# Sigmoid attention and token mixing on one core: a new written-out order, and copies split by PSUM bank

## The chip, the core and the metric

The kernel runs on one core of one Trainium2 chip. The metric is device time in microseconds (us) of one execution. A profile of one execution gives a span, from the first to the last instruction of the program; the execution's own time is a little longer. Engines are TensorE (PE in the profile, with its weight loads as PEld), VectorE (DVE), ScalarE (ACT), GpSimd (POOL) and SyncE (SP), whose queue issues nearly all transfers.

## What is computed

Batch 8, 12 heads, 448 tokens, head size 64, model width 768. Attention with a sigmoid in place of a softmax feeds a token mixer:

```
scores = scale * q @ k.T - log(448);  attn = sigmoid(scores);  x = attn @ v        # per head, x is (8, 448, 768)
wq, wk = x @ w_q, x @ w_k                                                          # (8, 448, 64)
W_tok  = scale * wq @ wk.T;  mixed = W_tok @ x
out    = relu(mixed) @ w_out                                                       # (8, 448, 768)
```

The kernel never forms W_tok: it multiplies wk by x first, a 64 by 768 matrix per batch entry ("tmp"), and that by wq.

## The kernel before, in words

Four heads of one batch entry make a quad; there are 24 quads, three for each of the eight batch entries u. For each quad q, k and v are loaded (448 KB each), cast to bf16 and, for q and k, transposed. The casts are mostly on POOL (L192, L202); the transposes are 32x32 block transposes on DVE (L232, L256, L263, with swaps of halves on POOL, L161 to L167) or matmuls with an identity (L216, L224).

Each quad has seven score steps S (`scores`, L294): four 64x64 matmuls of 448 columns that run side by side in the array's four quarters (L298), into two PSUM banks, and one sigmoid on ACT over 896 columns (L303). Seven value steps P (L320) accumulate attn times v; the last of them copies the sum out as xt (L329). A step x (`tr_x`, L342 or L358) transposes xt back into xn.

When the three quads of u are done the mixer of u follows: W (`mlp_wqk`), six products of xt and the two projection weights, either over the whole 128x128 array (L395, with a second copy wq by POOL or ACT at L404 or L402) or over its four quarters (L383, with two copies and an addition, L390 to L392); N, transposes of wk (L410); U or T, tmp (L424, or L439 in quarters, L443 and L444); M (`mlp_mix`, L463 or L474) and a relu on the way out of PSUM (`relu`, L446: ACT at L448 or DVE at L450). Then the output products O and I with w_out, in pairs w of batch entries: for w in TW = (1, 2) `out_pair` (quarters, L506, one copy out at L515); for w = 0 and 3 `out_chunk` (whole array, six matmuls to a half row block, L583, copy at L607) or `out_halves` (quarters, L542, L547 and L548). Outputs are stored from SP (L523, L556, L592).

Nothing of the order is left to a scheduler. `PLAN` (L132) is a string of 636 letters that the loop at L761 walks: S is a score step, P or p a value step, O or o a step of an output product, and so on; a small letter mostly puts the copy on ACT in place of DVE, and other letters choose other forms (`ALIKE`, L757). Every engine executes its instructions in the order in which the loop emits them. `BANKS` (L67) names the PSUM bank or pair of banks for each step that needs one. `ORDER` (L657) is the order of 77 loads: "w0" is the two projection weights, "w1" to "w6" the six blocks of the output weights. Loads go through a ring of eight buffers (`pump_loads`, L676), so a load is issued once the tile eight places before it in the ring has been cast; casts are given to POOL in the same order as soon as their buffers allow (`pump`, L717), save for the entries marked with a dot or a capital, which DVE or ACT takes (letters 1 and 2 in `PLAN`). The output weights are cast at L704.

Two letters decide where a copy runs:

```
read(fb, COPY["s" if act else "v"](out=o, in_=ps[:, :, 0:NB]), keep=True)    # out_pair: one engine, both banks
tail = done["S"] == N * NI                                                     # after the last score step
```

After the last score step `tail` is true, and then `values`, `tr_x` and the relu of `mlp_mix` outside TW split each copy by bank, one half on DVE and one on ACT.

Of the kernel before, what the change touches and what calls it, by code (L numbers as in the profile page):

```python
# [17 lines left out]
def kernel(  # L18
# [17 lines left out]
    P = 128  # L36
# [4 lines left out]
    NB = D // 2  # L41
# [6 lines left out]
    def pool(name, bufs, **kw):  # L48
# [16 lines left out]
    banks16 = banks.rearrange("p b x -> p (b x)").bitcast(BF16).rearrange("p (b x) -> p b x", b=8)  # L65

    BANKS = (  # L67
# [11 lines left out]
    )  # L79
    BANKS = BANKS.split()[::-1]  # L80

# [43 lines left out]
    def xt(u, j):  # L125
# [4 lines left out]


    PLAN = (  # L132
        "FFSSSKSSFaSbFFrSFFSFsFzFSSPSSpPpPpPpSSrSsPppSSPPPSxzSSSXSPrP"
        "SpSsPPPPzSWwwWSSwWXSPPNrpSppSPPSUSPSszSpppSqkpSpPSMSSMSxSxSM"
        "cdSPppPSSpPPWrSwWsWSSWWPpSXSPPpSPzPSOSOSxNSOSrsSOoSSOTzSSppp"
        "ppSSpProoSpSPpSPPpSsPWwzWoSWMSWoWSSMoOSNxSPcPSMPppSPdPSoCCOS"
        "SScXOCOSpdppSxCpPSpCPSUrSPPSPpSPPPSszoOSSSCOoXwwwSMSWoWSxSWO"
        "SMSpppcSppSdPPPcPpSPpPSPSoONSMSooxdSTSPPPSppPSPSOYoWWWWw1WSM"
        "OSocSONdSOmppppcpSoSpPdOSOSOSXXSmooSo1TcoSooSMOSOPPSPSpppSdP"
        "cOoSooMSPpPPp2SpPSWXWwwwWXmOSOSodOSOSoSocpSPOpSPdPSPPOSoSONS"  # L140
        "OSUSOS1MoSOMoPmpcdPPpPSPo1SOSoSOoSOxSoSOPSPppScPdSpOPOSoxSOc"
        "lLSlSlLLOdSOSoxSOppPSNppPSPpPSpppSPpTOSOSoxSOPPmpPpMPPmxWWWw"
        "wwxiNiitiiimmiiIMiIiOOoOOoOooOOooOoO"
    )
    KIND = ["a"] + [t for t in PLAN if t in "qacer"]

# [226 lines left out]
    wkn, tmps, mxs = {}, {}, {}  # L373
# [72 lines left out]
    def relu(fb, dst, ps, act):  # L446
        if act:
            inst = nc.scalar.activation(dst, ps, ACTF.Relu, bias=0.0, scale=moe_scale)  # L448
        else:
            inst = nc.vector.tensor_scalar(dst, ps, moe_scale, 0.0, ALU.mult, ALU.max)  # L450
        read(fb, inst)

    def mlp_mix(u, c, act, tail):
        w = u // 2
        if c == 0 and u % 2 == 0:
            mxs[w] = p_mx.tile([P, 2 * 12 * 256], BF16, tag="mx", name="mx")
        fb, ps, _ = bank2()
        wq = (wqks[u % 2], wq2s[u % 2])
        if w in TW:
            for z in range(2):  # L460
                for y in range(2):
                    for x in range(2):
                        nc.tensor.matmul(  # L463
                            ps[HALF[x], y, 256 * z : 256 * z + 256],
                            tmps[u][HALF[y], c * P + 64 * z : c * P + 64 * z + 64],
                            wq[y][HALF[y], 192 * x : 192 * x + 256], start=True, stop=True,
                        )
            relu(
                fb, mxs[w].rearrange("p (u y c x) -> p u c y x", u=2, y=2, c=3)[:, u % 2, c], ps, act
            )  # L470
            return
        for y in range(2):
            for x in range(2):
                nc.tensor.matmul(  # L474
                    ps[HALF[x], y, 0:S], tmps[u][HALF[y], c * P + 64 * x : c * P + 64 * x + 64],
                    wq[y][HALF[y], 0:S], start=True, stop=True,
                )
        mx = mxs[w][:, 0 : 12 * S].rearrange("p (y c u s) -> p c u y s", y=2, c=3, u=2)[:, c, u % 2]
        if tail:
            for y in range(2):  # L480
                relu(fb, mx[:, y], ps[:, y, 0:S], y)
        else:
            relu(fb, mx, ps[:, :, 0:S], act)
# [7 lines left out]

        return b // 2 + (0 if b % 2 == half else NC)

    def out_pair(act):

        if opened:
            w, blocks, part, fb, ps = opened.pop()
        else:
            w, blocks = chunks.pop(0)
            part = 0  # L500
            fb, ps, _ = bank2()
        mx = mxs[w].rearrange("p (u b x) -> p u b x", u=2, b=12)
        for b in range(3 * part, 3 * part + 3):
            for y, (u, i) in enumerate(blocks):
                for x in range(2):
                    nc.tensor.matmul(  # L506
                        ps[HALF[x], y, 0:NB], mx[HALF[y], u, b, 64 * (i - 3 * y) : 64 * (i - 3 * y) + 64],
                        wout16[HALF[y], slot(y, b), x * NB : (x + 1) * NB],
                        start=(b == 0), stop=(b == 11),
                    )  # L510
        if part < 3:
            opened.append((w, blocks, part + 1, fb, ps))
            return
        o = p_o.tile([P, 2, NB], F32, tag="o", name="o")
        read(fb, COPY["s" if act else "v"](out=o, in_=ps[:, :, 0:NB]), keep=True)  # L515
        (u0, i0), (u1, i1) = blocks
        for x in range(2):
            cols = slice(x * NB, (x + 1) * NB)
            if u0 == u1:
                dst = out[2 * w + u0].rearrange("(p i) d -> p i d", i=NI)[:, i0 : i1 + 1 : i1 - i0, cols]  # L520
            else:
                dst = out[2 * w : 2 * w + 2].rearrange("b (p i) d -> i p b d", i=NI)[i0, :, :, cols]
            nc.sync.dma_start(out=dst, in_=o[HALF[x]])  # L523
# [129 lines left out]
    for t in wqks:  # L653
# [1 line left out]


    ORDER = (  # L657
# [4 lines left out]
    )  # L662
    BY = {"s": [], "v": []}
    for x in ORDER.split():
# [89 lines left out]
    used |= {("q", 0), ("k", 0)}  # L754
    pump()

    ALIKE = dict(a="q", c="q", e="q", r="q", b="k", d="k", f="k", s="k", j="k", h="k", X="x", y="x", Y="x", g="g", z="z", L="W", l="W", T="U", t="U", I="O", i="O")  # L757
    done["q"] = done["k"] = 1
    quads_r = []

    for t in PLAN:  # L761
# [11 lines left out]
            scores(*divmod(c, NI))  # L773
        elif kind == "P":
            n, i = divmod(c, NI)
            values(n, i, tail, "s" if t == "p" else "v")
            if i == NI - 1:
                used.add(("v", n))
                pump()
# [11 lines left out]
        elif t == "g":  # L791
            move()
        elif t == "z":
            n = quads_r.pop(0)
            quadrants(n, 1)
            used.update({("q", n), ("k", n)})
            pump()
        elif t == "K":
            tr_part("k", k016, KB, "v")
        elif kind == "x":  # L800
            tr_x(c, tail, t in "XY", "s" if t in "yY" else "v")
        elif kind == "W":
            mlp_wqk(*divmod(c, NC), tail, t in "wl", t in "Ll")
        elif kind == "C":
            for y in range(2):
                nc.sync.dma_start(out=wout16[HALF[y], NC + c, :], in_=wout16[HALF[1 - y], c, :])
        elif kind == "N":
            mlp_wkn(c)
        elif kind == "U":
            (mlp_tmp_tiled if t in "Tt" else mlp_tmp)(c, t in "ut")  # L810
        elif kind == "M":
            u, x = divmod(c, NC // 2)
            mlp_mix(u, x, t == "m", tail)
            if x == NC // 2 - 1:
                if u // 2 in TW:
                    chunks.extend((u // 2, ((u % 2, i), (u % 2, 6 - i))) for i in range(3))
                    if u % 2:
                        chunks.append((u // 2, ((0, 3), (1, 3))))
                else:
                    chunks.extend((u // 2, m, -1) for m in (range(3, NI) if u % 2 else range(3)))  # L820
        elif kind == "O":
            if (opened or chunks)[0][0] in TW:
                out_pair(t == "o")
            elif t in "Ii":
                out_halves(t == "i")
            else:
                out_chunk(t == "o", tail)
    assert not chunks and not opened and not BANKS
# [1 line left out]
_INS = ['q', 'k', 'v', 'moe_w_q', 'moe_w_k', 'moe_w_out']  # L830
# [26 lines left out]
```

## Time and profile before

| what | us |
|---|---|
| median of three runs | 186.23 (184.76 to 186.94) |
| the profiled execution's own time | 185.52 |
| its span | 183.7 |
| busy: PE, ACT, DVE, POOL | 171.8, 162.0, 143.3, 125.3 |
| first sigmoid starts, last sigmoid ends | 7.04, 160.94 |
| loads and stores: moved, mean rate | 48.47 MB, 264 GB/s |

The granted TensorE clock was full (1.00) over the whole span. A line of the groups gives the source line, engine, operation, tiles (out<-in), shape and count, then busy time in us, the mean of one in ns and the idle time of the engine before them with what ended it. A busy PE is not a PE at its peak, since the ends of pipelined matmuls are modelled; four quarter matmuls that run side by side count once in busy time.

### The profile page before, as it was taken

Reading aid. Unit: us, or ns where it says so; the run is one execution under the profiler, and the core shown is the slowest. Engines: PE = TensorE matmul, PEld = TensorE weight load, DVE = VectorE, ACT = ScalarE, POOL = GpSimd, SP = SyncE. Lnnn points to the kernel's source line nnn. Section 1 sums busy time; section 2 is a strip of 40 time slices with the busy share of each in tenths; the row PEclk is TensorE's granted clock in tenths of the full one; section 3 lists DMA queues with packets and bytes.
Section 4 is the critical chain, followed back from the end, with each engine's and each line's share of the span. In section 5 each row is a group of like instructions: output and inputs, shape, how many; then the busy total and the mean of one; then the engine's idle time right before and its main releaser. Section 6 shows DMA issues by size and latency. Waiting matters only on the chain.

```text
span 183.7 us, 7643 instructions
## 1 busy us (share of the span) xinstructions
PE 171.8 (94%) x3313; PEld 111.0 (60%) x3314; DVE 143.3 (78%) x221; ACT 162.0 (88%) x208; POOL 125.3 (68%) x168
## 2 busy tenths in 40 slices
PE   7877799979999999999999999999999999999990
PEld 7433445444545446555665887867766778878650
DVE  3229999999999999888987976876587788596720
ACT  4599999999999989999999999999999999977330
POOL 1399887999972999999998999996999921000000
PEclk9999999999999999999999999999999999999999
DMA  5999999959999947898998778999759534231786
GB/s 175 332 404 397 324 343 403 397 192 329 364 409 386 340 131 266 274 305 259 316 295 269 207 268 241 390 372 370 227 127 304 171 92 107 69 88 27 177 232 171
DMA packets 24722, 48.47 MB, mean 264 GB/s; under 512 B 3952, under 2 KB 17264, under 8 KB 24688
## 3 DMA queue, kind: packets, MB, share of 16 engines
q1 hardware_dynamic: 24288, 47.20, 78.5%
q10 hardware_dynamic: 400, 0.79, 1.4%
q8 instruction: 26, 0.43, 0.9%
q14 instruction: 8, 0.07, 0.1%
HBM read 35.78 MB, written 11.01 MB: 255 GB/s over the span
## 4 chain that ended last, share of the span: by engine, by line
PE 64%; DVE 16%; ACT 10%; DMA 4%; POOL 1%; SPq 1%; issue 1%
PE banks L506 15%; PE banks L298 12%; PE banks L320 11%; ACT at L303 10%; PE banks L583 10%; DVE qk L232 6%; DMA q<-in_q_dram 4%; DVE qk L256 3%; PE banks L542 3%; PE banks L395 3%; DVE xt L329 3%; PE banks L342 2%; PE banks L358 2%; PE banks L463 1%; PE banks L439 1%; POOL qk L192 1%
## 5 line engine op out<-in xcount | busy, mean ns | idle before, releaser
L303 ACT ACTIVATE at<-banks 128x896 bf16<-128x896 f32 x168 | 140.2, 939 | 4.0 <-PE banks L298 3.1
L298 PE MATMUL banks<-qk 64*64 64x448 bf16 x672 | 62.9, 357 | 4.4 <-DVE xt L329 2.0
L320 PE MATMUL banks<-at,v 64*64 64x448 bf16 x672 | 45.9, 351 | 0.2
L298 PEld LDWEIGHTS <-qk 64*64 64x64 bf16 x672 | 26.4, 105 | 24.1 <-issue 15.5
L506 PE MATMUL banks<-wout,mx 64*64 64x384 bf16 x672 | 36.7, 323 | 0.0
L192 POOL CAST qk<-k 128x896 bf16<-128x896 f32 x20 | 23.9, 1195 | 6.8 <-DVE qk L232 4.7
L320 PEld LDWEIGHTS <-v 64*64 64x64 bf16 x672 | 23.8, 106 | 7.3 <-issue 1.5
L329 DVE CAST xt<-banks 128x896 bf16<-128x896 f32 x22 | 23.8, 1083 | 3.9 <-PE banks L320 3.5
L506 PEld LDWEIGHTS <-mx 64*64 64x64 bf16 x672 | 22.3, 107 | 5.8
L192 POOL CAST qk<-q 128x896 bf16<-128x896 f32 x20 | 24.9, 1250 | 0.8 <-DMA q<-in_q_dram 0.5
L583 PE MATMUL banks<-wout,mx 128*128 128x384 bf16 x132 | 25.0, 327 | 0.0
L232 DVE STREAM_TRANSPOSE qk<-qk 32x448 f32<-32x448 f32 x32 | 20.4, 636 | 0.8
L450 DVE TENSOR_SCALAR mx<-banks 128x1024 bf16<-128x1024 f32 (+2 forms) x20 | 19.7, 997 | 1.4 <-PE banks L463 1.2
L202 POOL CAST v<-v 128x896 bf16<-128x896 f32 x21 | 19.5, 935 | 1.1 <-DMA v<-in_v_dram 0.5
L583 PEld LDWEIGHTS <-mx 128*128 128x128 bf16 x132 | 11.7, 98 | 10.5 <-issue 3.7
L263 DVE STREAM_TRANSPOSE qk<-qk 128x448 f32<-128x448 f32 x26 | 16.1, 630 | 0.1
L161 POOL COPY swap<-qk 32x448 uint32<-32x448 uint32 x26 | 14.4, 556 | 2.2 <-DVE qk L192 0.7
L164 POOL COPY qk<-qk 32x448 uint32<-32x448 uint32 x26 | 14.4, 556 | 1.5
L167 POOL COPY qk<-swap 32x448 uint32<-32x448 uint32 x26 | 14.4, 554 | 1.5
L515 DVE COPY o<-banks 128x768 f32<-128x768 f32 x11 | 10.5, 955 | 5.3 <-ACT at L303 3.9
L371 DVE COPY xn<-banks 128x1024 bf16<-128x1024 bf16 (+1 forms) x14 | 9.1, 651 | 3.3 <-PE banks L358 3.2
L395 PE MATMUL banks<-xt,wqk 128*128 128x448 bf16 x42 | 10.8, 354 | 0.3 <-ACT at L303 0.3
(87 smaller groups left out, 188.0 us busy)
## 6 DMA issues: line engine op xcount, KB each, us to landing
q<-in_q_dram SPq DMA_DIRECT2D x24, 448.0 KB, 6.4
v<-in_v_dram SPq DMA_DIRECT2D x24, 448.0 KB, 7.7
k<-in_k_dram SPq DMA_DIRECT2D x23, 448.0 KB, 7.2
out_dram<-o SPq DMA_DIRECT2D x51, 192.0 KB, 3.7
w<-in_moe_w_out_dram SPq DMA_DIRECT2D x6, 384.0 KB, 6.8
wout<-wout SPq DMA_DIRECT2D x12, 96.0 KB, 6.4
out_dram<-o ACTq DMA_DIRECT2D x3, 192.0 KB, 3.3
k<-in_k_dram SPq DMA_DIRECT2D x1, 256.0 KB, 4.8
```

Source lines behind the costliest of these rows:

```text
L192: COPY[e](out=f[:, :, "qk".index(nm)].rearrange("p e i d y -> p e y i d"), in_=ld.pop((nm, n)).rearrange("p (y i e d) -> p e y i d", y=2, ...
L202: COPY[e](out=t16.rearrange("p i b d -> p b i d"), in_=ld.pop((nm, n)).rearrange("p b (i d) -> p b i d", i=NI),)
L232: nc.vector.transpose(out=qk[n][other : other + 32, h].rearrange("p t i n -> p (t i n)").bitcast(F32), in_=w[own : own + 32, 1 - h],)
L263: nc.vector.transpose(out=qk[n][:, t].rearrange("p t i n -> p (t i n)").bitcast(F32), in_=w)
L298: nc.tensor.matmul(sc[HALF[h], g, 0:S], qk[n][HALF[g], h, 1, i, :], qk[n][HALF[g], h, 0].rearrange("p i n -> p (i n)"), start=True, stop=True,
L303: inst = nc.scalar.activation(at, sc[:, :, 0:S], ACTF.Sigmoid, bias=attn_bias, scale=attn_scale)
L320: nc.tensor.matmul(ps[HALF[g], h, 0:S], ld["v16", n][HALF[h], i, g, :], ats[n, i][HALF[h], g, :], start=(i == 0), stop=(i == NI - 1),)
L329: read(fb, COPY[eng](out=xt(u, j)[:, :, 0:S], in_=ps[:, :, 0:S]))
L395: nc.tensor.matmul(ps, wqk16[:, c, :], xt(u, c // 2)[:, c % 2, 0:S], start=(c == 0), stop=(c == NC - 1),)
L450: inst = nc.vector.tensor_scalar(dst, ps, moe_scale, 0.0, ALU.mult, ALU.max)
L506: nc.tensor.matmul(ps[HALF[x], y, 0:NB], mx[HALF[y], u, b, 64 * (i - 3 * y) : 64 * (i - 3 * y) + 64], wout16[HALF[y], slot(y, b), x * NB : ...
L583: nc.tensor.matmul(ps, mxs[w][:, 2 * S * c + m * P : 2 * S * c + (m + 1) * P], wout16[:, c, w0:w1], start=(c == 0), stop=(c == NC - 1),)
```

## The change

`PLAN`, `BANKS` and `ORDER` are replaced as wholes, and three letters are new: Q is an output step whose copies are split by bank in `out_pair` (one half on DVE, one on ACT; in `out_chunk` it means ACT), G is a mixing step whose relu is split the same way, and R a value step whose copy is split. R is not used in the new `PLAN`. The functions called are the same but for the splits; in `mlp_mix` the split now covers the pairs in TW too, when G asks for it or after the last score step.

```diff
     PLAN = (
-        "FFSSSKSSFaSbFFrSFFSFsFzFSSPSSpPpPpPpSSrSsPppSSPPPSxzSSSXSPrP"
-        "SpSsPPPPzSWwwWSSwWXSPPNrpSppSPPSUSPSszSpppSqkpSpPSMSSMSxSxSM"
-        "cdSPppPSSpPPWrSwWsWSSWWPpSXSPPpSPzPSOSOSxNSOSrsSOoSSOTzSSppp"
...
-        "lLSlSlLLOdSOSoxSOppPSNppPSPpPSpppSPpTOSOSoxSOPPmpPpMPPmxWWWw"
-        "wwxiNiitiiimmiiIMiIiOOoOOoOooOOooOoO"
+        "FFSSKFSaSSFSbFFFSSSSFrsFPSSPPFPSzPPPPrSPPSPPsPSPSSXSSPPzSPPX"
+        "SwwSrPPPSWSwSSqszWkSwXSPPPSPPNPSPSUSXSMMSSPPSMSPcPSdPPPSOSOS"
+        "SOrOSSOsOzSSOOSIrCSISPPsPPSPPzpwWwSSwXISISwwXSSPPPNcPPPPSSUP"
...
+        "PSOSONSOQxSOSOcSdOPSPOSPPPPSPOSOxSOQPSSPPTPyPPLpLLmLyLmlOMOO"
+        "xNoITiIIIGiIMimOOOOOOOoOoOoOQOOOoOO"
     )
@@ mlp_mix
-            relu(
-                fb, mxs[w].rearrange("p (u y c x) -> p u c y x", u=2, y=2, c=3)[:, u % 2, c], ps, act
-            )
+            mx = mxs[w].rearrange("p (u y c x) -> p u c y x", u=2, y=2, c=3)[:, u % 2, c]
+            if tail:
+                for y in range(2):
+                    relu(fb, mx[:, y], ps[:, y], y)
+            else:
+                relu(fb, mx, ps, act)
             return
@@ out_pair
-    def out_pair(act):
+    def out_pair(act, split):
...
-        read(fb, COPY["s" if act else "v"](out=o, in_=ps[:, :, 0:NB]), keep=True)
+        if split:
+            for y in range(2):
+                read(fb, COPY["vs"[y]](out=o[:, y], in_=ps[:, y, 0:NB]), keep=True)
+        else:
+            read(fb, COPY["s" if act else "v"](out=o, in_=ps[:, :, 0:NB]), keep=True)
@@ ORDER
-        "q1 k1 q2 k2 v0 v1 k3 q3 v2 q4 k4 v3 w0 q5 k5 q6 v4 k6 q7 k7 k8 v5 v6 q8 w4 w1 w6 w2 w3 "
-        "w5 q9 k9 v7 k10 q10 v8 k11 q11 v9 k12 q12 v10 v11 k13 q13 q14 v12 k14 v13 k15 q15 q16 "
...
+        "q1 k1 k2 q2 v0 q3 v1 k3 v2 w0 q4 k4 k5 q5 v3 k6 w2 q6 v4 w1 w4 w3 w6 w5 k7 q7 k8 q8 v5 "
+        "v6 q9 k9 v7 k10 q10 k11 v8 q11 q12 v9 k12 v10 v11 q13 k13 k14 v12 q14 q15 k15 k16 v13 "
...
@@ the loop over PLAN
-            values(n, i, tail, "s" if t == "p" else "v")
+            values(n, i, tail or t == "R", "s" if t == "p" else "v")
...
-            mlp_mix(u, x, t == "m", tail)
+            mlp_mix(u, x, t == "m", tail or t == "G")
...
-                out_pair(t == "o")
+                out_pair(t == "o", t == "Q")
...
-                out_chunk(t == "o", tail)
+                out_chunk(t in "oQ", tail)
```

In the built programs the first output product stands behind 39 score steps on PE, where it stood behind 51. The six casts of output weights stand between the 21st and the 27th sigmoid in the emitted order, where they stood between the 35th and the 38th. Projections in quarters (L, l) are 24 of the 48 steps W, where they were 6; transposes x over the whole array (X, Y) are 14, where they were 10.

More of the change, by code (lines that the diff above doesn't have):

```diff
@@ L132 @@
     PLAN = (
-        "FFSSSKSSFaSbFFrSFFSFsFzFSSPSSpPpPpPpSSrSsPppSSPPPSxzSSSXSPrP"
-        "SpSsPPPPzSWwwWSSwWXSPPNrpSppSPPSUSPSszSpppSqkpSpPSMSSMSxSxSM"
-        "cdSPppPSSpPPWrSwWsWSSWWPpSXSPPpSPzPSOSOSxNSOSrsSOoSSOTzSSppp"
[L136 to L141, printed above, removed]
-        "lLSlSlLLOdSOSoxSOppPSNppPSPpPSpppSPpTOSOSoxSOPPmpPpMPPmxWWWw"
-        "wwxiNiitiiimmiiIMiIiOOoOOoOooOOooOoO"
+        "FFSSKFSaSSFSbFFFSSSSFrsFPSSPPFPSzPPPPrSPPSPPsPSPSSXSSPPzSPPX"
+        "SwwSrPPPSWSwSSqszWkSwXSPPPSPPNPSPSUSXSMMSSPPSMSPcPSdPPPSOSOS"
+        "SOrOSSOsOzSSOOSIrCSISPPsPPSPPzpwWwSSwXISISwwXSSPPPNcPPPPSSUP"
+        "dSPMSCPPPGCGPSPScXOSdSSOOOSPPPSSPrPPPsSOwSCwwwSSwWOSPNPPSSPP"
+        "PzPSXXSPPPSPPSCPcSPCOOSxSdTPSPPSPPPPSwWOcSMSWOWSxSOSdMowwSxP"
+        "PSPcPPSdPSPrOQSMSNOoXSSsPPPPPSPPOSOSzSxOScOSUSdSPMPPSPPPSPOS"
+        "OSMOSQLlclSLlSLPPPSPPPSPOSO1dSOQSMPPPSPPPSPOSOSOcSdSOXXSPPSN"
+        "PPPSPPlSLlcLtLlSOOSdOGSOSXXSPP1PSPPPSPOSOSMOSQOScOdNm1OSxQTS"
+        "PPSPPPPSp1OMcOSOQSdSOOOSPPSOPPSPPPSOGOScO1LSOdmLLLLSLPPPPSPP"
+        "PSOSONSOQxSOSOcSdOPSPOSPPPPSPOSOxSOQPSSPPTPyPPLpLLmLyLmlOMOO"
+        "xNoITiIIIGiIMimOOOOOOOoOoOoOQOOOoOO"
     )
@@ L755 @@
     pump()
-    ALIKE = dict(a="q", c="q", e="q", r="q", b="k", d="k", f="k", s="k", j="k", h="k", X="x", y="x", Y="x", g="g", z="z", L="W", l="W", T="U", t="U", I="O", i="O")
+    ALIKE = dict(a="q", c="q", e="q", r="q", b="k", d="k", f="k", s="k", j="k", h="k", X="x", y="x", Y="x", g="g", z="z", L="W", l="W", T="U", t="U", I="O", i="O", Q="O", G="M", R="P")
     done["q"] = done["k"] = 1
```

26 rows, old and new, of tables (BANKS, ORDER) are left out of this document.

## The prediction

> **What bounds the kernel now.** I read the page's shares first, then windows of the sigmoid stream, then the chain of waits at the end, then groups by line.
>
> ```profile
> span 183.7 us, 7643 instructions
> PE 171.8 (94%) x3313; PEld 111.0 (60%) x3314; DVE 143.3 (78%) x221; ACT 162.0 (88%) x208; POOL 125.3 (68%) x168
> ```
>
> PE looks like the bound, but the share hides two stages. The windows (us, then busy us and instructions of PE, PEld, DVE, ACT, POOL, then clock, DMA share, GB/s) are cut at the first sigmoid's start and, within 0.1 us, the last one's end:
>
> ```profile
> 7.04:160.84 153.80, 147.13 (x2945) 93.61 (x2942) 128.90 (x184) 149.51 (x183) 123.66 (x161) 1.00 0.86 285
> 160.84:183.70 22.86, 18.64 (x328) 12.65 (x320) 12.14 (x24) 9.98 (x22) 0.00 (x0) 1.00 0.53 140
> ```
>
> ACT is busy 149.51 of 153.80 us in the first and idle 4.29. What it does there, by group (busy, mean ns, idle before):
>
> ```profile
> L303 ACT ACTIVATE at<-banks 128x896 bf16<-128x896 f32 x168 | 140.2, 939 | 4.0 <-PE banks L298 3.1
> L448 ACT ACTIVATE mx<-banks 128x1024 bf16<-128x1024 f32 x4 | 4.1, 1028 | 0.5 <-PE banks L463 0.5
> L607 ACT COPY o<-banks 128x384 f32<-128x384 f32 x8 | 4.0, 494 | 4.5 <-PE banks L583 4.5
> L515 ACT COPY o<-banks 128x768 f32<-128x768 f32 x3 | 2.4, 800 | 0.7 <-ACT at L303 0.4 <-PE banks L506 0.3
> L347 ACT COPY xn<-banks 128x1024 bf16<-128x1024 bf16 x1 | 1.0, 1043 | 0.0
> L202 ACT CAST v<-v 128x896 bf16<-128x896 f32 x1 | 0.9, 939 | 0.0
> L329 ACT CAST xt<-banks 128x896 bf16<-128x896 f32 x1 | 0.9, 924 | 0.0
> ```
>
> So the first stage is paced by ACT: 140.2 us for 168 sigmoids is 0.834 each. After the last sigmoid the chain of waits (start, us, what) is PE without a hole, to the last copies:
>
> ```profile
> 159.87 0.49 PE banks L506 x12
> 160.75 0.19 PE banks L474 x4
> 160.94 0.57 PE banks L320 x12
> 162.54 1.29 PE banks L395 x6
> 163.83 0.37 PE banks L358 x32
> 165.84 0.74 PE banks L439 x14
> 166.57 1.46 PE banks L542 x36
> 171.57 7.92 PE banks L583 x48
> 179.52 0.37 DVE o L604
> ```
>
> Two stages in series, then: a stream paced by ACT, and what PE still has to do behind the last score product. A change helps if it shortens the stream or leaves less behind it.
>
> **The change part by part.** Counts are from the instruction orders of the two built programs.
>
> ACT before the last sigmoid. Before: the groups above, with five of the eight L607, sum to 4.11 + 5 x 0.494 + 2.40 + 1.04 + 0.94 + 0.92 = 11.89 us. New: two 896-column copies (0.924), seven halves of output copies, three output copies of L607's form, two whole relus, two relu halves of 448 columns and two of 512, three copies into wq, one wpart and one upart copy. Their rows:
>
> ```profile
> L547 ACT COPY o<-banks 128x384 f32<-128x384 f32 x6 | 2.9, 480 | 1.0 <-PE banks L474 0.5 <-PE banks L542 0.5
> L448 ACT ACTIVATE mx<-banks 128x448 bf16<-128x448 f32 x6 | 3.2, 549 | 0.6 <-PE banks L474 0.5
> L402 ACT CAST wq<-banks 64x448 bf16<-64x448 f32 x1 | 0.5, 525 | 0.9 <-DVE wqk L400 0.9
> L443 ACT COPY upart<-banks 128x384 f32<-128x384 f32 x1 | 0.5, 479 | 0.5 <-PE banks L439 0.5
> ```
>
> 1.85 + 7 x 0.480 + 3 x 0.494 + 2 x 1.028 + 2 x 0.549 + 2 x 0.60 (between 549 and 1028 ns by columns) + 3 x 0.525 + 0.525 + 0.479 = 13.63 us. The stream carries **+1.74 us** of ACT work.
>
> PE behind the last score product. Before, in the chain's prices: L506 x12 0.49, L320 x28 1.33, L474 x24 1.14, L358 x64 0.74, L395 x6 1.29, L439 x14 0.74, L542 x144 5.84, L583 x48 7.92: 19.49, beside 8 small L410 that both orders have. The chain's own stretch, 159.87 to 179.49, is 19.6, so these prices leave nothing out. New: L506 x48 1.96, L320 x24 1.14, L474 x24 1.14, L358 x96 1.11, L383 x24 at L474's price (the same 64x64 by 448) 1.14, L439 x28 1.48, L542 x96 3.89, L583 x60 9.90: 21.76. The tail carries **+2.27 us**: four steps of 64x64 output products (48 of L542) have left it for the start of the stream, but another tmp product (14 of L439), three steps of L506 and four of L583 now lie behind the last score product.
>
> ACT's idle time. Of the 4.29 us some 0.5 lies at the start, where scores are late:
>
> ```profile
> 12.39 1.77 ACT L303 ACTIVATE at<-banks 128x896 bf16<-128x896 f32 x2 [0.38 <-PE banks L298]
> 30.15 10.16 ACT L303 ACTIVATE at<-banks 128x896 bf16<-128x896 f32 x12 [0.15 <-PE banks L298]
> ```
>
> The rest comes late, where PE has no room:
>
> ```profile
> 30.00:50.00 20.00, 18.41 (x377) 9.76 (x370) 19.63 (x29) 19.73 (x25) 19.27 (x24) 1.00 0.91 327
> 100.00:160.00 60.00, 60.00 (x1459) 46.02 (x1461) 44.86 (x62) 57.77 (x71) 43.27 (x61) 1.00 0.73 231
> ```
>
> PE has 1.59 us free in 30 to 50 and none in 100 to 160, where ACT idles 2.23. The new order puts 24 + 48 output matmuls ahead of the 64th sigmoid instead of 18: 5.9 us against 3.0 in the prices above. This is the gain the change can have: late PE lateness bought off with early PE room. I let a third of the idle go, 1.4 us. Bounds: nothing goes (there are eight more ACT instructions that can each wait for a product), or all but the start's 0.5 goes (3.8). I take the value nearer the first, since both splits make ACT wait for PE's output groups, as L448 and L515 do in 1.2 us of waits for seven instructions.
>
> POOL and SP. The six casts of output weights move from 35 to 38 sigmoids into the stream to 21 to 27, their loads some eleven sigmoids up on SP's queue, past the loads of quads 7 and 8:
>
> ```profile
> 0.00:47.12 47.12, 36.34 (x49) 1.00 0.94 329
> 30.65 10.20 SPq L624 DMA_DIRECT2D w<-in_moe_w_out_dram  x6
> 42.42 4.70 POOL L704 CAST wout<-w 128x768 bf16<-128x768 f32 x6
> L192 POOL CAST qk<-k 128x896 bf16<-128x896 f32 x20 | 23.9, 1195 | 6.8 <-DVE qk L232 4.7 <-DVE qk L263 1.6 <-DMA k<-in_k_dram 0.2
> L202 POOL CAST v<-v 128x896 bf16<-128x896 f32 x21 | 19.5, 935 | 1.1 <-DMA v<-in_v_dram 0.5
> L404 POOL COPY wq<-wqk 64x448 bf16<-64x448 bf16 x6 | 3.3, 556 | 0.4
> L256 DVE STREAM_TRANSPOSE qk<-qk 128x448 f32<-128x448 f32 x16 | 9.4, 623 | 1.0 <-POOL qk L192 0.8
> L232 DVE STREAM_TRANSPOSE qk<-qk 32x448 f32<-32x448 f32 x32 | 20.4, 636 | 0.8
> ```
>
> The sixth cast has four L192 casts, two L202 and one L404 fewer ahead of it: 4.78 + 1.87 + 0.56 = 7.2 us, so it ends near 47.12 - 7.2 = 39.9 if POOL idles as now. The first output product stands behind the 39th sigmoid's scores, near 7 + 38 x 0.834 = 38.7 to 39.7, and its second half, which needs the sixth cast, one sigmoid on: there is no room, but no loss either. Quad 7's casts then end at 42.3, its six transposes (2 x 0.623 + 4 x 0.636 = 3.8) at 46.1, its scores are wanted at 7 + 49 x 0.834 = 47.9 less 0.5: 1.3 us of cover. I price the move at nothing; if that cover goes, ACT waits one for one.
>
> DVE. It gets the other halves of the split copies and relus and three more wqk additions for whole copies and transposes that go, and it has 153.80 - 128.90 = 24.9 us idle in the stream: no charge. Uncovered, an instruction more costs what its ACT twin does, 0.5 us.
>
> Mode changes on PE. Scores after a 128x128 product take longer:
>
> ```profile
> 73.12 0.97 PE banks L583 x6
> 74.10 0.31 PE banks L298 x4
> 74.98 0.19 PE banks L298 x4
> ```
>
> 0.12 us more. The new order changes between array shapes 82 times, not 76; up to the 112th sigmoid ten more, where PE waits for ACT, afterwards four fewer. No charge; uncovered, ten cost 1.2 us. The Trainium skill (TensorEngine Tiling (Array Packing), Key Properties) says that changing the tiling mode drains TensorE. The 0.12 us agrees with that.
>
> **Sum.** +1.74 + 2.27 - 1.4 = +2.6 us: span 186.3, and with the 1.8 us around the span (185.52 against 183.7) 188.1. The median of the three runs, 186.23, stands 0.7 above this execution and the lowest, 184.76, 0.8 below; I keep the execution's own base.
>
> **The rivals.**
> Output weights late (slower still): POOL, already busy 19.27 of 20 us in 30 to 50, waits for loads that now queue where DMA is near full. PE executes in order, so a late sixth cast stops scores too, and quad 7's cover of 1.3 us goes. It decides from 1.3 us of POOL delay; a whole 4.7 us block late costs 3.4, giving 191.5. Against: the two cast rows above show 0.7 us of waits for loads in 41 casts.
> ACT stays fed (not slower): idle falls to the start's 0.5, because PE is 3 us ahead in output products from the 64th sigmoid on. Then +1.74 + 2.27 - 3.8 = +0.2: 185.7. For: the late idle sits where PE was full. Against: more waits per copy.
> Steadier sigmoids (faster): fed without breaks they run closer together,
>
> ```profile
> 36.96 13.07 ACT at L303 x16
> ```
>
> 0.817 each against 0.834. Over 168 that is -2.9; with the idle at 0.5 too, +0.2 - 2.9 = -2.7: 182.8. It decides only if both hold, and against it stand 23 interposed ACT instructions where there were 15.
> The Trainium skill (Perfetto Trace Analysis, Identifying the Most-Contended Engine) would judge by occupancy for ScalarE but not by matmul busy time for TensorE. By that rule ACT's +1.74 alone would count, 187.3; the tail rows above, PE without a hole for 20 us, contradict it.
>
> **How the numbers follow.** Forecast 0.50, output weights late 0.18, ACT stays fed 0.20, steadier sigmoids 0.12. The forecast's own range, idle 0.5 to 4.29, is 185.7 to 189.5. The range for 8 in 10 leaves out most of the fastest case and the end of the slowest: 184.3 to 190.8. About 1% (1.9 us) is what a measurement can tell. Slower by over 1%: 0.37 of the forecast's 0.50 and all 0.18, 0.55. Within 1%: 0.13 of the forecast and 0.17 of the fed case, 0.30. Faster: 0.12 + 0.03 = 0.15.
>
> **What would show it.** Last sigmoid's end near 161.2 (160.84 + 1.74 - 1.4); PE behind the last score product near 21.9 us, not 19.6; ACT idle in the stream about 2.9; the sixth cast at about 39.9 and the first output product near 39. Wrong if the last sigmoid ends before 159, or the tail stays at 20.

## The result, and the profile after

The new order takes **186.94 us** (median of 20 runs; 185.62 for the kernel before beside it), a ratio of **1.0069 [1.0042, 1.0096]**: some 1.3 us slower, which is within 1%. The forecast was 188.1, and of its two likelier classes, slower by over 1% (0.55) and within 1% (0.30), the less likely one came. That it can be told from no change at all is owed to the 20 runs of each. The profiled execution took 186.8 us.

The shares of the page, then the two windows (us, then busy us and instructions of PE, PEld, DVE, ACT, POOL, then clock, DMA share, GB/s) cut at the first sigmoid's start and the last one's end:

```profile
span 185.0 us, 7589 instructions
PE 172.1 (93%) x3270; PEld 114.5 (62%) x3272; DVE 141.8 (77%) x226; ACT 162.7 (88%) x216; POOL 127.6 (69%) x172
```

```profile
6.48:160.83 154.35, 147.29 (x2880) 96.08 (x2879) 127.27 (x187) 149.89 (x192) 125.49 (x164) 1.00 0.86 282
160.83:185.00 24.17, 19.67 (x350) 14.44 (x341) 12.21 (x25) 10.32 (x21) 0.56 (x1) 1.00 0.57 146
```

The stream is 0.4 us longer (154.33 against 153.89) but starts 0.56 sooner, so the last sigmoid ends about where it did. The whole loss shows behind it: 24.17 us against 22.86. In the stream ACT is busy 149.89 (149.51 before) and idle 4.46. ACT's groups there (busy, mean ns, idle before) and what it waited for (total, times, longest; the wait ahead of the first sigmoid, 1.0 us before and 0.8 after, is counted in, and waits under 0.15 us are not):

```profile
L303 ACT ACTIVATE at<-banks 128x896 bf16<-128x896 f32 x168 | 140.1, 955 | 2.7 <-PE banks L298 2.5
L448 ACT ACTIVATE mx<-banks 128x448 bf16<-128x448 f32 (+2 forms) x6 | 4.4, 746 | 0.0
L520 ACT COPY o<-banks 128x384 f32<-128x384 f32 x7 | 3.7, 527 | 0.1
L402 ACT CAST wq<-banks 64x448 bf16<-64x448 f32 x3 | 1.6, 524 | 2.3 <-DVE wqk L400 2.3
```

```profile
ACT at L303 <- PE banks L298: 2.5, 6, 0.8
ACT wq L402 <- DVE wqk L400: 2.3, 3, 1.1
```

Idle time did not fall, it changed its owner. Waits for scores went from 3.1 us to 2.5, and the waits at L448 and L515 (1.2 us) are gone (0.1 us is left at L520); but the three copies into wq now wait 2.3 us for DVE, where there was no such copy on ACT in the stream before. The rows in order of time show how (start, duration, what, idle before):

```profile
29.20 1.09 DVE L286 COPY qk<-banks 128x1792 bf16<-128x1792 bf16 x1
30.21 0.61 DVE L400 CAST wqk<-banks 128x448 bf16<-128x448 f32 x1
30.86 0.52 ACT L402 CAST wq<-banks 64x448 bf16<-64x448 f32 x1 [1.06 <-DVE wqk L400]
```

Both L400 and L402 read the one bank in which the projection lies, and in the program ACT's read comes behind DVE's: it was L400 that released L402 all three times. DVE is still at a 1.09 us copy, so ACT, with a sigmoid queued behind L402, stands for 1.06 us. The Trainium skill (PSUM — Partial Sum Buffer, PSUM bank collisions raise a hardware error) says that two engines may not read the same bank and quadrant at once, and that the hardware does not arbitrate. The trace agrees in so far as the two never overlap; no run here took that wait away alone (experiment 8 takes the copy with it).

POOL, SP and PE around the output weights, then the chain of waits at the end:

```profile
27.88 0.83 POOL L711 CAST wout<-w 128x768 bf16<-128x768 f32 x1
34.56 3.91 POOL L711 CAST wout<-w 128x768 bf16<-128x768 f32 x5
39.93 0.66 PE L590 MATMUL banks<-wout,mx 128*128 128x384 bf16 x3
19.05 0.60 SPq L631 DMA_DIRECT2D w<-in_moe_w_out_dram  x1
24.24 4.08 SPq L631 DMA_DIRECT2D w<-in_moe_w_out_dram  x5
```

```profile
158.82 0.38 PE banks L298 x8
159.20 0.38 PE banks L320 x8
159.58 0.64 PE banks L439 x14
166.09 0.57 PE banks L439 x14
170.64 9.87 PE banks L590 x60
180.59 0.37 DVE o L611
180.98 0.32 ACT o L612
```

The sixth cast ends at 38.47 (34.56 + 3.91) instead of 47.12, with no wait of ACT between 31 and 54. Behind the last scores PE works from 159.20 to 180.51, 21.3 us, where it was 19.6.

**What the sigmoids cost.** I paired the starts of all neighbouring sigmoids in both traces:

| pairs of sigmoids | before | after |
|---|---|---|
| back to back | 140, 113.98 us (0.814 each) | 141, 114.21 us (0.810) |
| broken by a late score | 14, 15.97 us, of it 2.71 idle | 6, 7.40 us, of it 1.74 idle |
| with other ACT work between | 13 (15 instructions), 22.97 us, 1.52 idle | 20 (23 instructions), 31.79 us, 2.70 idle |

A broken pair takes 0.95 us without its idle time, 0.13 more than one back to back: eight fewer are worth 1.0 us. The faster pitch is worth 0.6. The instructions between cost (21.45 - 13 x 0.814) = 10.9 us before and (29.1 - 20 x 0.814) = 12.8 after, so +1.95. The three sum to +0.3, which is why ACT's busy time hardly rose. This is read from one execution of each kernel. Why the pitch is closer no run shows; in the traces of the new order with the wq copies off ACT, or with whole copies, it is 0.814 to 0.817, as before.

### The profile page after: what moved, and what is told of

Its sections match the earlier page's. It is cut to its first block, busy times and chain, and to the rows that moved or that the text cites. A ratio compares the mean times of both kernels' runs of the same rounds, so it can differ in the third digit from the quotient of the medians.

```text
span 185.0 us, 7589 instructions
## 1 busy us (share of the span) xinstructions
PE 172.1 (93%) x3270; PEld 114.5 (62%) x3272; DVE 141.8 (77%) x226; ACT 162.7 (88%) x216; POOL 127.6 (69%) x172
## 4 chain that ended last, share of the span: by engine, by line
PE 60%; DVE 17%; DMA 9%; ACT 8%; issue 2%; POOL 1%; SPq 1%; DVEq 0%; ACTq 0%
PE banks L509 12%; PE banks L298 12%; PE banks L320 11%; PE banks L590 10%; ACT at L303 7%; DMA k<-in_k_dram 7%; DVE qk L232 5%; PE banks L342 2%; DVE qk L256 2%; DMA out_dram<-o 2%; PE banks L549 2%; PE banks L383 2%; PE banks L439 2%; PE banks L358 1%; DVE mx L450 1%
## 5 line engine op out<-in xcount | busy, mean ns | idle before, releaser
L320 PE MATMUL banks<-at,v 64*64 64x448 bf16 x672 | 47.6, 351 | 0.9 <-DVE o L522 0.4
L192 POOL CAST qk<-q 128x896 bf16<-128x896 f32 x19 | 23.0, 1212 | 6.2 <-DVE wkn L416 2.4
L509 PEld LDWEIGHTS <-mx 64*64 64x64 bf16 x672 | 24.5, 107 | 4.5 <-issue 0.5
L202 POOL CAST v<-v 128x896 bf16<-128x896 f32 x23 | 21.7, 953 | 1.9 <-DMA v<-in_v_dram 1.4
L450 DVE TENSOR_SCALAR mx<-banks 128x448 bf16<-128x448 f32 (+3 forms) x22 | 20.2, 928 | 2.9 <-PE banks L463 1.9
L232 DVE STREAM_TRANSPOSE qk<-qk 32x448 f32<-32x448 f32 x28 | 17.8, 636 | 0.8
L164 POOL COPY qk<-qk 32x448 uint32<-32x448 uint32 x28 | 16.0, 572 | 1.6
L392 POOL COPY wq<-wqk 64x448 bf16<-64x448 bf16 x4 | 2.2, 556 | 13.7 <-DVE wqk L391 13.6
L614 DVE COPY o<-banks 128x384 f32<-128x384 f32 x13 | 7.2, 553 | 5.7 <-PE banks L590 5.5
L347 DVE COPY xn<-banks 128x1024 bf16<-128x1024 bf16 x14 | 9.3, 682 | 0.7 <-PE banks L342 0.6
```

The source lines that it names most:

```text
L164: eng.tensor_copy(out=w[hi, 0], in_=w[lo, 1])
L192: COPY[e](out=f[:, :, "qk".index(nm)].rearrange("p e i d y -> p e y i d"), in_=ld.pop((nm, n)).rearrange("p (y i e d) -> p e y i d", y=2, ...
L202: COPY[e](out=t16.rearrange("p i b d -> p b i d"), in_=ld.pop((nm, n)).rearrange("p b (i d) -> p b i d", i=NI),)
L232: nc.vector.transpose(out=qk[n][other : other + 32, h].rearrange("p t i n -> p (t i n)").bitcast(F32), in_=w[own : own + 32, 1 - h],)
L320: nc.tensor.matmul(ps[HALF[g], h, 0:S], ld["v16", n][HALF[h], i, g, :], ats[n, i][HALF[h], g, :], start=(i == 0), stop=(i == NI - 1),)
L509: nc.tensor.matmul(ps[HALF[x], y, 0:NB], mx[HALF[y], u, b, 64 * (i - 3 * y) : 64 * (i - 3 * y) + 64], wout16[HALF[y], slot(y, b), x * NB : ...
```

## The experiments

Ratios are to the kernel before, run on the same chip beside each. "Stream" is from the first sigmoid's start to the last one's end; idle is ACT's in it. Streams, waits and rows are those of one profiled execution. In experiments 2, 3, 6 and 7 that execution took 1.1 to 2.4 us more than the median, so the size of a loss is read from the ratio there. The executions of one kernel differ: those of the kernel before mostly lie between 184.7 and 187.6 us.

**1. Copies into wq on POOL.** The new order with three letters of `PLAN`:

```diff
-...SSqszWkSwXSP... ...XISISwwXSSP... ...SdMowwSxP
+...SSqszWkSWXSP... ...XISISwWXSSP... ...SdMowWSxP
```

> The new kernel with its three copies into wq on POOL (556 ns each there) in place of ACT, where they take 1.6 us and wait 2.3 us behind DVE's copy out of the same bank. Theory A, the sigmoid stream is paced by ACT and the PE tail stands behind it in series: the last sigmoid ends 2.5 to 3.9 us earlier than 160.8 and the span falls to 181.1 to 182.5, below the kernel before. Theory B, PE is full from 100 us on and would only wait less for ACT before that and more after: the last sigmoid ends less than 1 us earlier, ACT's idle time grows behind sigmoid 100 by what was saved, the span stays above 184.

Measured: 196.19 us, ratio 1.0483 [1.0410, 1.0557]: neither theory. The last sigmoid ends at 170.1, far behind 160.8. PE's waits (total, times, longest), and POOL's rows ahead of the first of them:

```profile
PE banks L477 <- POOL wq L404: 9.7, 2, 7.5
```

```profile
34.19 0.93 POOL L202 CAST v<-v 128x896 bf16<-128x896 f32 x1
35.07 3.90 POOL L711 CAST wout<-w 128x768 bf16<-128x768 f32 x5
38.93 1.17 POOL L192 CAST qk<-k 128x896 bf16<-128x896 f32 x1
40.02 1.17 POOL L192 CAST qk<-q 128x896 bf16<-128x896 f32 x1
41.25 0.56 POOL L404 COPY wq<-wqk 64x448 bf16<-64x448 bf16 x1
```

ACT copied wq at 30.86 in the new order; POOL gets to it at 41.25, since it works without a pause on what stands ahead in its queue, 3.90 us of that the casts of output weights. PE executes in order, so the mixing product that wants wq holds the scores too (ACT's longest wait for one is 8.0 us). The granted clock was 0.50 in 40 to 42 us and 0.56 in 42 to 46; what this adds was not separated. So in the new order the wq copy cannot stay on POOL where it stands. That the early output weights alone make it late is not shown: in experiment 6 it also comes behind them, at 35.88, and PE does not wait for it.

**2. Copies into wq on ACT, in the order before.**

```diff
-...PzSWwwWSSwWXSP... ...SwWsWSSWWPpSX... ...SWoWSxSWO
+...PzSWwwWSSwwXSP... ...SwWsWSSWwPpSX... ...SWoWSxSwO
```

> The kernel before with the wq copies of batch entries 0, 1 and 3 moved from POOL to ACT, as the new order has them. Theory A: ACT gains 1.6 us of copies and about 2.3 us of waits for DVE's copy of the same bank, the time rises by 2.5 to 3.9 us (1.4 to 2.1%). Theory B: the kernel before is held by PE late, so the time rises by under 1 us.

Measured: 188.51 us, ratio 1.0120 [1.0083, 1.0156], +2.2 us. Stream 158.08, busy 151.40 (+1.8), idle 6.68 (+2.4).

```profile
ACT wq L402 <- DVE wqk L400: 1.1, 2, 0.7
```

The 2.2 us lie between the theories, nearer to A's lower end of 2.5: with nothing else changed, three copies on ACT cost more than their own 1.6 us. But their waits for DVE in the stream come to 1.1 us, not the 2.3 that A took over from the new order, and one of the three copies did not wait.

**3. Copies of products and relus whole.** The new order with each Q made O and each G made M ahead of the last score step.

> The new kernel without the splits inside the stream: its seven split output copies (Q) and four split relus (G) go whole to DVE. ACT loses 7 x 0.48 + 2 x 0.60 + 2 x 0.57 = 5.7 us of short copies, DVE gains about 11 x 0.4 = 4.4 us. Theory A: the stream shortens by 2 to 5 us where nothing else waits; the span falls to 180 to 183. Theory C, the splits earn their ACT time by freeing PSUM banks 0.4 us sooner: PE and then the sigmoids wait longer for the banks, and the span stays within 1 us of 185.0 or rises.

Measured: 190.92 us, ratio 1.0240 [1.0178, 1.0301]. ACT has 3.0 us less to do in the stream (146.87) and idles 8.0 us more (12.43):

```profile
ACT at L303 <- PE banks L298: 9.6, 19, 1.2
```

Nineteen late scores, where there were six. This is theory C, and more. In this order the splits are worth far more than the ACT time that they take: about 3 us by the ratios (1.0240 against 1.0069).

**4. Fewer output products, in the new order.** It leaves out two of the four steps of every `out_pair` product up to the last score step, so PE has less to do and nothing else differs; the sums of those outputs lack terms.

```diff
-        for b in range(3 * part, 3 * part + 3):
+        for b in range(3 * part, 3 * part + 3) if part in (0, 3) or done["S"] == N * NI else ():
```

> The new kernel leaves out the two middle steps of every output product of batch entries 2 to 5 that stands before the last score step: 24 matmuls, about 0.98 us of PE, for each of 13 products, 12.7 us of PE in all, nothing on ACT, DVE or the queues. Theory A: the stream is ACT's, so its end moves only by the idle time that PE lateness now causes behind the 100th sigmoid, 1 to 1.5 us, and the span falls to 183 to 184.5. Theory B: the stream is PE's from 100 us on and ends 4 us or more earlier.

**5. The same cut in the kernel before.** It leaves out the same steps.

> The kernel before leaves out the two middle steps of every output product of batch entries 2 to 5 that stands before the last score step, as was done in the new order (about 0.98 us of PE for each product). The new order's stream ended 1.7 us shorter by that. If the earlier output products bought off waits for PE, the kernel before waits more and its stream shortens by 2.5 to 3.7 us; if they bought nothing, by the same 1.7 us or less.

Measured, one run of each: 185.7 us for the new order and 183.14 for the kernel before, spans 183.9 and 181.4. The windows of the stream, the new order's first:

```profile
6.50:159.20 152.70, 140.53 (x2560) 84.55 (x2561) 126.54 (x187) 148.54 (x191) 125.32 (x164) 1.00 0.86 285
```

```profile
7.00:159.00 152.00, 140.15 (x2614) 83.97 (x2618) 128.91 (x185) 148.97 (x184) 123.86 (x160) 1.00 0.86 287
```

PE's busy time falls by some 7 us in both, and the stream gets shorter by only 1.69 us (154.33 to 152.64) in the new order and by 2.10 (153.89 to 151.79) in the one before. So the stream is ACT's (theory A of experiment 4), and what the cut gives back is 1.7 and 2.1 us. By this the early output products have bought off 0.4 us and not 1.4; but the 2.10 lies between the two readings that were written down for it (1.7 or less; 2.5 to 3.7), and 0.4 us between single executions cannot be told from nothing.

**6. Early output weights, in the order before.** `ORDER` alone is changed:

```diff
-... v4 k6 q7 k7 k8 v5 v6 q8 w4 w1 w6 w2 w3 w5 q9 ...
+... v4 k6 w4 w1 w6 w2 w3 w5 q7 k7 k8 v5 v6 q8 q9 ...
```

> The kernel before with one thing of the new order alone: the loads and casts of the six blocks of output weights stand ahead of those of q and k of quad 7, as they do in the new order; output products stay where they were. Theory: POOL's 4.7 us of weight casts then stand ahead of the wq copy of batch entry 0 and of quad 7's casts, the mixing step waits for wq and, PE being in order, the scores with it; ACT's idle time before the 50th sigmoid rises by 1 to 4 us and the time by as much. Rival, the casts and loads are hidden wherever they stand: within 0.7 us of the kernel before.

**7. The same, with the first wq copy on ACT.** Besides, `...SSwWXSPPNrp...` is made `...SSwwXSPPNrp...`.

> The same early weights in the kernel before, and the wq copy of batch entry 0 on ACT instead of POOL, as the new order has it. Theory: the wait at the mixing step goes and ACT pays 0.5 us plus about 1 us of wait for DVE's copy of the same bank; the time lies 1 to 2 us above the kernel before, and below the run with the copy left on POOL if that one lost more than 1.5 us. Rival: no better than with the copy on POOL.

Measured: 189.88 us, ratio 1.0213 [1.0138, 1.0287], and 189.42 us, 1.0207 [1.0132, 1.0283]. ACT's longest wait is 3.50 us at 46.8 in the first and 3.36 at 47.4 in the second, so the wq copy was not what waited; the rival of experiment 7, no better with it on ACT, holds. PE's longest wait in the first, and POOL's rows there:

```profile
PE banks L320 <- POOL v L202: 2.6, 1, 2.6
```

```profile
42.56 1.18 POOL L192 CAST qk<-k 128x896 bf16<-128x896 f32 x1
43.65 1.81 POOL L202 CAST v<-v 128x896 bf16<-128x896 f32 x2
```

The value step waits until the first of these v casts is done, near 44.6. The block of weight casts has pushed it back; in the kernel before, these two casts stand at

```profile
39.56 1.81 POOL L202 CAST v<-v 128x896 bf16<-128x896 f32 x2
```

The granted clock was 0.50 in 44 to 48 us of the first; what it adds to the loss was not separated. This is the rival "output weights late", by another victim: moving the loads and casts of the output weights alone costs about 4 us. The new order has no ACT wait there; which of its other edits it owes that to was not tested.

**8. Copies into wq on DVE, in the new order.** DVE copies them too, ahead of what it does next:

```diff
-            if tail or act:
+            if tail:
                 read(fb, nc.scalar.copy(out=w2[HALF[1]], in_=ps[HALF[0]]))
+            elif act:
+                nc.vector.tensor_copy(out=w2[HALF[1]], in_=w[HALF[0], 0:S])
```

> The new kernel with its three copies into wq inside the stream on DVE, right behind DVE's own copy out of the bank and reading that copy from SBUF, so that ACT has neither the copy (0.52 us each) nor the wait for DVE (0.58 to 1.06 us each) and POOL's full queue isn't used. Theory A, the stream is ACT's: the last sigmoid ends 2 to 3.9 us earlier than 160.8, the span falls to 181 to 183, the time lies 1 to 2% below the new kernel and at or below the kernel before. Rival: DVE, over 90% busy until 70 us, passes the delay on to the scores, and the span stays above 184.3.

Measured: 185.85 us, ratio 0.9970 [0.9933, 1.0006]. A second set of runs of the same kernel:

> The new order with ACT's three wq copies given to DVE, once more, for a profile and a closer interval. By the first timing 185.85 against 185.96 for the kernel before: theory A, ratio 0.990 to 1.001, the three waits (2.3 us) and three copies (1.6 us) come off the stream and PE's lateness takes about half back: stream 152 to 153.5, idle 3 to 4.5. Rival B, the gain was the chip's: ratio 1.004 to 1.010 as for the new order, stream above 154.

Measured: 185.89 us, ratio 0.9991 [0.9955, 1.0027]. Stream and waits:

```profile
6.42:160.01 153.59, 146.77 (x2882) 95.87 (x2879) 128.77 (x190) 148.87 (x189) 125.56 (x164) 1.00 0.86 284
```

```profile
ACT at L303 <- PE banks L298: 4.9, 11, 1.0
```

Theory A by the ratio, which is 0.8 to 1.0% below the new order's. In the trace it gets less than it said: stream and idle time (4.72) lie just above its ranges, and the last sigmoid ends 0.8 us earlier, not 2 to 3.9. ACT is 1.0 us less busy and the 2.3 us of waits for DVE are gone, but waits for scores grow from 2.5 to 4.9 us. Of these 1.5 us lie at the second and third sigmoid (0.98 at 9.1 and 0.54 at 10.6), where nothing was changed.

**9. That kernel with fewer output products.** It leaves out the same two of four steps as experiment 4.

> The kernel with ACT's wq copies given to DVE, and besides two of the four steps of every output product left out before the last score (as in the two runs that cut them before). Theory A, with the three waits for DVE gone the stream is limited by ACT's own work and late PE costs what it cost the new order (1.7 us): stream about 150.5 to 151, span about 181.5 to 182. Theory B, ACT's time away from wq was handed to late scores, PE is the next limit: the cut brings 2.5 us or more against the undisturbed run of the kernel without the cut, and the idle time of ACT falls below 3 us. The run beside it of the same kernel without the cut is the one to compare with.

Measured: one run of 184.57 us.

```profile
6.62:158.48 151.86, 139.77 (x2570) 84.97 (x2567) 128.24 (x190) 148.12 (x188) 125.03 (x164) 1.00 0.86 287
```

The stream falls by 1.73 us (153.59 to 151.86), though it is still an us longer than expected, and idle time is 3.74, not below 3. That is theory A's size, as in the new order: PE has not become the limit.

**10. A shorter tail.** The new order, whose last output products leave out one of six chunks, 10 matmuls of 60:

```diff
-            for c in range(c0, c1):
+            for c in range(c0, c1) if not tail else [c for c in range(c0, c1) if c != 1]:
```

> The new order, in which the last output products leave out one of their six chunks (10 of the 60 matmuls at the end; nothing else differs). Theory A, the end behind the last scores is one chain on PE, so the 1.7 us that it grew by are paid in full: the 60 matmuls took 9.87 us, 0.165 each, so the last matmul ends 1.65 us sooner and the span falls from 185.0 to about 183.4, the stream of sigmoids (154.3) unchanged. Rival B, the copies or the stores of the output set the end: the span falls by less than 0.6 us.

Measured: span 183.4, one run of 185.23 us. The matmuls at the end (minimum, median and maximum ns, first and last start), here and in the new order:

```profile
L590 PE MATMUL banks<-wout,mx x50: 326/326/337, 170.3 to 178.3; 128*128 128x384 bf16 x50
```

```profile
L590 PE MATMUL banks<-wout,mx x60: 326/326/336, 170.6 to 180.2; 128*128 128x384 bf16 x60
```

From the end of the last score product to the end of the last matmul it is 19.7 us instead of 21.3, 1.6 less, and the span falls by 1.6. The tail is paid in full, as theory A says. How much more could be had in this way is open: in the shortened tail ACT's copies wait 2.6 us for stores of earlier outputs, and the chain that ends last runs from 169.8 us on through copies and a 3.70 us store instead of PE.

**11. Splits alone, in the order before.** Seven of the fourteen copies of `out_pair` products are split (letters o or O made Q, with the new code of `out_pair`; three of the seven letters are shown).

```diff
-...o1TcoSooSMOSOPPSPSpppSdP cOoSooMSPp...
+...o1TcQSooSMOSQPPSPSpppSdP cOoSoQMSPp...
...
-                out_pair(t == "o")
+                out_pair(t == "o", t == "Q")
```

> The kernel before, of the change only the copies of output products split by bank over DVE and ACT, at 7 of its 14 product copies in the stream (3 that ACT made whole and 4 that DVE made whole). Theory A, a copy in halves frees its banks some 0.45 us sooner (955 ns whole on DVE, about 500 a half), and that is worth more than the ACT time (4 halves of 0.53 added, 3 whole copies halved, +0.8 us): idle 4.3 falls by over 1 us, ratio 0.993 to 1.0. Rival B, in this order nobody waits for those banks, since it was planned with whole copies: the ACT time is paid, ratio 1.003 to 1.008.

Measured: 186.57 us, ratio 1.0031 [0.9999, 1.0062]; stream 155.20 (+1.3), busy 150.07 (+0.5), idle 5.12 (+0.8).

```profile
ACT at L303 <- PE banks L298: 3.4, 8, 1.1
ACT mx L448 <- PE banks L463: 1.1, 1, 1.1
```

Theory A is not borne out: the idle time rose in this execution, and a gain is all but outside the interval. That reaches from no change to just beyond rival B's middle, so the size stays open. (The ACT time written down for it, +0.8, is +1.3 by its own terms: 4 x 0.53 less 3 x 0.27.) What experiment 3 found was found in an order that was written around splits; this order shows nothing of it.

## Why the prediction was right in size, and where its steps failed

**ACT work, +1.74: the price held, the term did not.** The instructions between sigmoids cost 1.95 us more, near the 1.74. But ACT's busy time rose by 0.3 to 0.4, because the sigmoids themselves got 1.6 us cheaper: fewer pairs broken by a late score, and a closer pitch. The cheaper sigmoids are a part of the rival "steadier sigmoids" (which put it at 2.9), and I had made it depend on the idle time going too. It does not: fewer and longer stalls cost as much idle time and break fewer pairs. Adding durations from a table of groups leaves out what an added or a removed stall does to its neighbours.

**ACT idle, -1.4: wrong, +0.2.** This is the step that failed: the sum had no term for what stands in the idle time's place. Idle time other than at the wq copies did fall, from 4.28 to 2.15 us (4.46 less 2.31), by more than the 1.4. But how much of that is late PE bought off stays open. With the wq copies on DVE (experiment 8) ACT idles 4.72 us, 1.5 of it in the first sigmoids, so a part of the late products was probably only hidden while ACT stood for DVE; experiments 4 and 5 give 0.4 us, which is not clear of noise. For the case that nothing goes I had named the wrong cause. It was not the split copies that wait for products: L520 waits 0.1 us in all. It was the three copies into wq, which I had priced at 0.525 each without a wait, although the row that I quoted for them (L402, "0.9 <-DVE wqk L400") carried one. Experiment 8 shows their price in the end: with them on DVE the ratio falls from 1.0069 to 0.9991 (0.9970 in the first set of runs), some 1.4 to 1.8 us, and the new order is as fast as the one before; that it is faster is not shown.

**The tail, +2.27: right in kind, +1.69 in size.** PE has no hole there, and experiment 10 shows that its microseconds count. Most of the difference lies in my prices: 14 of L439 took 0.57 and 0.64 where I took 0.74, and the L358 0.9 in all where I took 1.11. Besides, the tail begins earlier: the last score product ends 1.61 us ahead of the last sigmoid's end, where it was 1.07, and I had no term for that. Both repeat: with the tail uncut, all traces of the order before and its variants have 19.6 to 19.7 us from the last score product to the last matmul, those of the new order 21.3 (21.6 in experiment 3). The sum over the stages: last sigmoid's end -0.13 (first sigmoid -0.56, stream +0.44), that lead -0.54, tail +1.69, copies and stores behind the last matmul +0.27, together +1.29. The -0.56 is in part the execution's: the first sigmoid starts between 6.58 and 7.04 us in the traces of the order before and its variants, between 6.27 and 6.95 in those of the new one.

**POOL and SP, nothing: right.** The sixth cast ended at 38.5 (39.9 forecast), the first product came at 39.9 (39). That it was right depended on what else moved: experiments 1, 6 and 7 show a wait of PE of 2.6 to 7.5 us when one piece of the arrangement is changed without the others. The rival's mechanism is real, and 1.3 us of cover was the right thing to look at, but for the v casts too, not only for quad 7.

**DVE, no charge: half wrong.** No run shows a cost of DVE's added copies by their length, but its place in the chain did cost: ACT stood behind DVE's queue three times.

**Mode changes, no charge.** No run tested them. Nor were `BANKS`, the projections in quarters or the transposes varied by themselves.

**The bound.** The Trainium skill (Perfetto Trace Analysis, Identifying the Most-Contended Engine) led to 187.3, and the time came out nearer to that than to my 188.1. Yet the cause is not the one it would give: ACT's busy time in the stream rose by 0.4 us, and experiment 10 moves the end by taking only PE work away.

Against the profiled execution (186.8) the forecast was 1.3 us too high: the work term by 1.5, the tail by 0.6 and its earlier start by 0.5, and 0.6 for a first sigmoid that I had not moved; against that the idle term was 1.6 too low and the copies and stores at the end 0.3. It came out near because the misses had both signs: that is luck, and in the stream above all, where work and idle time missed by 1.5 and 1.6 in opposite directions.

## What to carry to other kernels

An instruction that moves to the pacing engine brings its wait along: look at what stands ahead of its producer in the other engine's queue, and take the idle time in its row into the price. Count the breaks in a run of the pacing engine as well as its idle time, since each costs both neighbours (here 0.13 us). In an order that is written out by hand the parts of a change hold each other up, so a part that is harmful or useful alone says little on the whole: the splits were worth about 3 us in the one order and showed no gain in the other.

## What was not expected of the hardware

- Sigmoids that follow a stall take 0.95 us to the next start, without the stall itself, against 0.81 back to back.
- A copy of 384 columns between two sigmoids adds 0.34 to 0.55 us, in most places less than its own row (0.48 to 0.61 us), which overlaps its neighbours' rows.
- The first quads' waits differ between executions of the same instructions: 0.25 us in the new order, 1.60 in experiment 10, whose program is the same up to the tail. Yet the streams of the two agree (154.33 and 154.11): the later waits were 1.1 us shorter and ACT's busy time 0.4. By these two executions a microsecond lost early was won back later.
